# Reordering the first tiles of a layer-norm stage: one maximum earlier, one later, one product-weight step on GpSimd

## Chip, cores and metric

One core of a Trainium2 chip runs the whole program. The metric is the device time of one execution in microseconds. The median of three runs of the kernel before is 331.34 us (331.23 to 331.82).

## What is computed

The reference has three stages; only the last one is touched. x (3072 x 512) is what the two stages ahead (chunked attention, then a soft mixture of experts) give.

```python
h = x @ w_in                                   # 3072 x 1024
e = np.exp(h - h.max(-1, keepdims=True))
sm = e / (e.sum(-1, keepdims=True) + 1e-09)
solu = h * sm
mu = solu.mean(-1, keepdims=True)
var = ((solu - mu) ** 2).mean(-1, keepdims=True)
ln = (solu - mu) / np.sqrt(var + 1e-06) * g_ln
return ln @ w_out                              # 3072 x 512
```

## The kernel before

The last stage works on 24 tiles of 128 tokens, numbered from 0. For every tile the steps are these; the names in italics are used from here on, and a number behind them in brackets is the tile.

- *h*: two products of 512 columns on TensorE (L659), into one of two PSUM pairs h0 and h1, by turns. A pair is free again when *u* of the tile two before has read it.
- *max* on VectorE (L665), *e* (the exponential, with its sum) on ScalarE (L668), *u* (h times e, with its sum) on VectorE (L674).
- *y*, the affine step that takes the mean off: on VectorE for tiles 1 and 2 (L688), halves on VectorE and ScalarE for tile 0 (L688, L692), on GpSimd for tile 3 (L690), on ScalarE from tile 4 on (L694).
- *sq* on ScalarE (L697), then *var* and *rstd* on GpSimd (L701 to L713, eleven small instructions), for the scale of the output row.
- y has to be transposed. For tiles 0 to 3 TensorE does it (L716, eight products into the PSUM tile t). From tile 4 on y goes through DRAM: a *store* of 512 KB (L722), four *fetch* transfers of 128 KB (L727), both issued on SP, and a *turning* on VectorE (L730).
- The transposed y is split into a high part, *hi* on ScalarE (L737), and a low part, *lo* on VectorE (L741), for accuracy.
- The *products* (L747): 24 of 128 x 512 per tile into one PSUM bank, eight of them yh by w_out's high part (whi), eight yh by its low part (wlo), eight yl by whi. The first ten of a tile are five pairs (whi, wlo); the eleventh is the first that needs lo.
- *out* on ScalarE (L765) and a write of 256 KB on SP (L766).

w_out comes in eight blocks. Each is unpacked by seven steps, of which the last two are the high part on ScalarE (L636) and the low part on VectorE (L640); the eighth block's steps are the entries `l` of the hand-written list `TAIL`, which orders the work up to tile 0's low parts. Behind it the function `final` orders everything: each step gets a time (`FRONT[n]` plus an offset of `OFF` for the steps up to y and the statistics, `HS[n]` for h, `begin[n]`, from which the products of a tile start, for the rest), and the steps are issued in the order of these times. The times are only sort keys; an engine takes its own instructions in that order, and waits for others by semaphores. An instruction that waits holds up all that stand behind it on its engine, on SP as well. Tiles beyond the tables get `front` from `begin` less `LEAD`.

Lines that matter: L52 and L53 (the tables), L57 (the list), L629 to L643 (the steps of w_out), L775 to L820 (`final`).

Of the kernel before, what the change touches and what calls it, by code (L numbers as in the profile page):

```python
# [7 lines left out]
FP32 = mybir.dt.float32  # L8
# [5 lines left out]
ALU = mybir.AluOpType  # L14
# [19 lines left out]
FC = FF // P  # L34
# [14 lines left out]
NCONST = 425  # L49
NPE, NZ = 4, 4  # L50
T0, TPE, TDM, TF, LEAD, TT, TO, TH = 6.2, 6.85, 5.51, 3.0, 16.3, 3.8, 6.3, 2.2
FRONT = (0.0, 5.5, 8.1, 15.5, 15.1)  # L52
HS = (0.0, 1.2999999999999998, 4.8, 10.3, 12.9)  # L53
YON = 'daddp'
OFF = {'max': 0.25, 'e': 1.7, 'u': 3.3, 'y': 3.6, 'sq': 5.25, 'var': 5.75, 'rstd': 10.0, 'yt': -2.6, 'hi': -2.1, 'lo': -0.1, 'st': 3.65, 'fe': 7.75, 'tr': 0.0, 'hi2': 0.45, 'lo2': 3.95, 'mh': 0.68, 'ml0': 3.4, 'ml': 0.21, 'l0': 0.7, 'l1': 7.25}

TAIL = (  # L57
    "so open l l l min l l e12 ha hb max s0 s1 t0 e keep w0 u t1 y0 y1 l w1 yt0 hi0 yt1 hi1 lo0 l lo1 e3"
).split()

SPR = ("pp", "ap")
# [17 lines left out]
def tile_kernel(ctx: ExitStack, tc: tile.TileContext, kr, vr, w1, w2, w_in, w_out, cst, out):  # L79
    nc = tc.nc  # L80
    pe, dve, act, pool, sp = nc.tensor, nc.vector, nc.scalar, nc.gpsimd, nc.sync
# [60 lines left out]
    g_sb = at("cst", C_G, FC)  # L142
# [22 lines left out]
    whi, wlo = {}, {}  # L165
# [336 lines left out]
    def c4t(i):  # L502
        return at(f"c4t{i // 12}", i % 12 * P, P, FP32R)
# [125 lines left out]
    def wout_ops(j, t):  # L629

        w = wo[t % len(wo)]

        def hi():
            area(f"w{j}", [(f"wh{j}", DM), (f"wl{j}", DM)])
            whi[j], wlo[j] = at(f"wh{j}", 0, DM, FP32R), at(f"wl{j}", 0, DM, FP32R)
            act.activation(out=whi[j], in_=w, func=ACTF.Copy, scale=g_sb[:, j:j + 1])  # L636

        return cast_ops(slot_of["wout", j], at("tmp", 512 * (t % 2), 512), w, dve) + [
            hi,
            lambda: dve.scalar_tensor_tensor(  # L640
                out=wlo[j], in0=w, scalar=g_sb[:, j:j + 1], in1=whi[j].bitcast(FP32), op0=ALU.mult, op1=ALU.subtract
            ),
        ]  # L643
# [7 lines left out]
    def sc(name, i):  # L651
        k = ("nm", "s", "nu", "vs", "x", "t", "r").index(name)
        o = 64 + 16 * (i % 8) + k
        return small[:, o:o + 1]

    def emit_h(i, halves=(0, 1)):
        for half in halves:
            sl = slice(512 * half, 512 * half + 512)
            pe.matmul(  # L659
                out=fin["h"][i % 2][:, sl], lhsT=c4t(i) if i else at("c0", 0, P), rhs=m4[:, sl] if i else mps[:, sl],  # L660
                start=True, stop=True,
            )
# [112 lines left out]
    def final():  # L775

        steps = []

        def put(t, f, *args):
            steps.append((t, len(steps), f, args))  # L780

        begin = [T0]
        for n in range(NTILE):
            begin.append(begin[-1] + (TPE if n + 1 < NPE else TDM))
        front = list(FRONT)
        for n in range(len(front), NTILE):
            front.append(max(front[-1] + TF, begin[n] - LEAD))
        for n in range(NTILE):
            a, b = front[n], begin[n]
            w = OFF  # L790
            if n >= 1:
                put(HS[n] if n < len(HS) else a - TH, emit_h, n)
                put(a + w["max"], emit_max, n)
                put(a + w["e"], emit_e, n)
                put(a + w["u"], emit_u, n)
                put(a + w["y"], emit_y, n)
            put(a + w["sq"], emit_sq, n)
            put(a + w["var"], emit_var, n)
            put(a + w["rstd"], emit_rstd, n)
            if 1 <= n < NPE:  # L800
                for f in range(FC):
                    put(b + w["yt"], emit_yt, n, f)
                put(b + w["hi"], emit_hi, n)
                put(b + w["lo"], emit_lo, n)
            if n >= NPE:
                put(a + w["st"], emit_store, n)
                put(a + w["fe"], emit_fetch, n)
                put(b - TT + w["tr"], emit_turned, n)
                put(b - TT + w["hi2"], emit_hi, n)
                put(b - TT + w["lo2"], emit_lo, n)  # L810
            if n == NTILE - 1:
                put(b + w["l0"], emit_last, n, 0)
                put(b + w["l1"], emit_last, n, 1)
                continue
            for f in range(FC):
                put(b + w["mh"] * f, main_hi, n, f)
                put(b + w["ml0"] + w["ml"] * f, main_lo, n, f)
            put(b + TO, emit_out, n)
        for t, _, f, args in sorted(steps, key=lambda x: x[:2]):
            f(*args)  # L820

    with tc.manual_schedule():
# [34 lines left out]
        for j in range(NEARLY):  # L857
# [4 lines left out]
            out=sel, in_=ident.rearrange("p (t s) -> p t s", t=4)[:, 0:GT, :], axis=AX.X, op=ALU.add  # L862
# [125 lines left out]
        def e3():  # L988
# [3 lines left out]

        bufs = {}
        last = wout_ops(FC - 1, 1)
        calls = dict(
            so=m_so, open=open_final, min=m_in, l=lambda: last.pop(0)(),
        )
        first = TAIL.index("e12")
        for x in TAIL[:first]:
# [3 lines left out]
        ob = [at("ob", 512 * i, 512) for i in range(3)]  # L1003
        sq = at("sq", 0, 1024)
        calls.update(
            h0=lambda: emit_h(0), ha=lambda: emit_h(0, (0,)), hb=lambda: emit_h(0, (1,)), max=lambda: emit_max(0), s0=lambda: m_sum(0), s1=lambda: m_sum(1),
            keep=lambda: keep_clock(fin["o"][1], KEEP[3]), t0=lambda: m_top(0), t1=lambda: m_top(1),
            w0=lambda: m_low(0), w1=lambda: m_low(1), e=lambda: emit_e(0), u=lambda: emit_u(0),
            y0=lambda: emit_y(0, 0), y1=lambda: emit_y(0, 1),
            yt0=lambda: [emit_yt(0, f) for f in range(4)], yt1=lambda: [emit_yt(0, f) for f in range(4, 8)],  # L1010
            hi0=lambda: emit_hi(0, 0), hi1=lambda: emit_hi(0, 1), lo0=lambda: emit_lo(0, 0), lo1=lambda: emit_lo(0, 1),
            e3=e3,
# [71 lines left out]
```

## Time and profile before

| what | value |
|---|---|
| median of three runs | 331.34 us |
| the profiled execution | 331.76 us |
| its span, first to last instruction | 330.0 us |
| TensorE busy | 298.8 us (91%) |
| VectorE busy | 236.9 us (72%) |
| ScalarE busy | 222.5 us (67%) |
| GpSimd busy | 169.1 us (51%) |
| granted TensorE clock | 1.00 |
| products L747 | 552, 129.8 us, mean 390 ns |

The last stage fills the time from about 174 us to the end. A product's 390 ns is its latency; products follow each other faster than that. Idle time of an engine only costs something where TensorE has to wait for it.

### The profile page before, as it was taken

The numbers are of one execution on the slowest core, as the hardware profiler recorded it, in microseconds if no ns is written. First come the engines' busy times: TensorE is split into PE (matmuls) and PEld (weight loads), VectorE is DVE, ScalarE is ACT, GpSimd is POOL, SyncE is SP. The second block draws the span as 40 slices with busy tenths as digits, with TensorE's granted clock in tenths as the row PEclk, the third lists the DMA queues.
The fourth block names the chain that finished last, engine by engine and source line by source line (L and its number), as shares of the span: only waits on it lengthen the run. The fifth ranks groups of instructions, "written<-read, shape, count | busy, mean of one in ns | idle before, by whom it ended". The sixth has DMA issues, their size and how long they took to land.

```text
span 330.0 us, 8289 instructions
## 1 busy us (share of the span) xinstructions
PE 298.8 (91%) x3069; PEld 217.0 (66%) x3069; DVE 236.9 (72%) x431; ACT 222.5 (67%) x441; POOL 169.1 (51%) x395
## 2 busy tenths in 40 slices
PE   2787989898898799879899899999999999999996
PEld 2576767677676433333335688888888888888885
DVE  6675888886877339998027986888878788787540
ACT  3566756865775446785326789998888888888721
POOL 5255577666675022233100457777767676666600
PEclk9999999999999999999999999999999999999999
DMA  7999999999999999999930005675656756576521
GB/s 291 422 368 411 412 415 420 413 420 414 416 403 412 392 422 428 422 423 423 422 148 0 1 34 195 240 264 199 234 218 219 251 203 219 219 237 238 194 95 65
DMA packets 32696, 95.85 MB, mean 290 GB/s; under 512 B 3856, under 2 KB 14480, under 8 KB 28944
## 3 DMA queue, kind: packets, MB, share of 16 engines
q1 hardware_dynamic: 32512, 95.11, 74.0%
q8 instruction: 24, 0.39, 0.5%
q10 hardware_dynamic: 144, 0.22, 0.2%
q14 instruction: 16, 0.13, 0.1%
HBM read 78.53 MB, written 16.78 MB: 289 GB/s over the span
## 4 chain that ended last, share of the span: by engine, by line
PE 61%; DMA 18%; DVE 9%; POOL 3%; issue 3%; ACT 2%; SPq 1%; POOLq 0%; ACTq 0%; DVEq 0%
PE bank L747 37%; DMA kq_area<-in_kr_dram 9%; DMA ex_area<-in_w_dram 5%; PE bank L281 5%; PE bank L337 4%; DMA e_area<-in_w_dram 4%; PE h L659 4%; POOL kq_area L330 3%; PE bank L319 2%; SPq L201 1%; PE bank L348 1%; PE bank L360 1%; PE bank L407 1%; PE bank L524 1%; PE bank L757 1%
## 5 line engine op out<-in xcount | busy, mean ns | idle before, releaser
L747 PE MATMUL bank<-wh_area,yh_area 128*128 128x512 f32 x552 | 129.8, 390 | 0.0
L747 PEld LDWEIGHTS bank<-wh_area,yh_area 128*128 128x128 f32 x552 | 103.4, 188 | 21.7
L330 POOL TENSOR_SCALAR kq_area<-kq_area 64x416 f32<-64x416 f32 x88 | 38.3, 440 | 36.2 <-DMA kq_area<-in_kr_dram 21.1
L281 PE MATMUL bank<-kq_area 128*32 128x128 f32 x768 | 29.4, 288 | 14.3 <-POOL kq_area L330 7.3
L322 ACT COPY s_area<-bank 128x384 f32<-128x384 f32 x32 | 15.3, 477 | 32.7 <-PE bank L319 31.4
L730 DVE STREAM_TRANSPOSE yq_area<-yq_area 128x1024 f32<-128x1024 f32 x20 | 24.9, 1245 | 17.2 <-DMA yq_area<-z 17.2
L674 DVE SCALAR_TENSOR_TENSOR eb_area<-h,eb_area 128x1024 f32<-128x1024 f32 x24 | 29.1, 1217 | 9.5 <-ACT eb_area L668 9.2
L281 PEld LDWEIGHTS bank<-kq_area 128*32 128x32 f32 x768 | 20.6, 114 | 20.6 <-POOL kq_area L330 10.7
L299 DVE TENSOR_REDUCE cst_area<-bank 128x6 f32<-128x384 f32 x32 | 17.8, 555 | 19.5 <-PE bank L281 19.0
L337 PE MATMUL bank<-vz_area,s_area 128*32 128x130 f32 x768 | 28.7, 274 | 3.3 <-issue 1.2
L712 POOL TENSOR_SCALAR cst_area<-cst_area 128x1 f32<-128x1 f32 x72 | 26.6, 370 | 7.6
L665 DVE TENSOR_REDUCE cst_area<-h 128x1 f32<-128x1024 f32 x24 | 29.0, 1217 | 0.9 <-PE h L659 0.9
L701 POOL TENSOR_SCALAR cst_area<-cst_area 128x1 f32<-128x1 f32 x24 | 16.9, 705 | 22.4 <-ACT eb_area L668 20.5
L668 ACT ACTIVATE eb_area<-h,cst_area 128x1024 f32<-128x1024 f32 x24 | 26.7, 1112 | 1.9 <-DVE cst_area L665 1.9
L697 ACT ACTIVATE eb_area<-eb_area,cst_area 128x1024 f32<-128x1024 f32 x24 | 27.3, 1139 | 0.1
L694 ACT ACTIVATE eb_area<-eb_area,cst_area 128x1024 f32<-128x1024 f32 x20 | 23.1, 1154 | 4.8 <-DVE eb_area L674 4.3
L741 DVE TENSOR_TENSOR yh_area<-yq_area,yh_area 128x1024 fp32r<-128x1024 f32 x20 | 24.5, 1226 | 2.3 <-ACT yh_area L737 2.3
L337 PEld LDWEIGHTS bank<-vz_area,s_area 128*32 128x32 f32 x768 | 21.6, 108 | 5.8 <-issue 2.2
L737 ACT CAST yh_area<-yq_area 128x1024 fp32r<-128x1024 f32 x20 | 21.0, 1049 | 5.4 <-DVE yq_area L730 5.3
L713 POOL TENSOR_SCALAR cst_area<-cst_area 128x1 f32<-128x1 f32 x72 | 19.9, 276 | 7.1
L765 ACT ACTIVATE eb_area<-bank,cst_area 128x512 f32<-128x512 f32 x23 | 15.8, 687 | 9.7 <-POOL cst_area L703 7.0
L314 ACT ACTIVATE s_area<-s_area 128x384 f32<-128x384 f32 x32 | 16.9, 530 | 2.4 <-DVE s_area L305 2.3
(153 smaller groups left out, 526.9 us busy)
## 6 DMA issues: line engine op xcount, KB each, us to landing
e_area<-in_w_dram SPq DMA_DIRECT2D x15, 1024.0 KB, 10.4
kq_area<-in_kr_dram SPq DMA_DIRECT2D x32, 400.0 KB, 7.3
vz_area<-in_vr_dram SPq DMA_DIRECT2D x32, 390.0 KB, 6.6
ex_area<-in_w_dram SPq DMA_DIRECT2D x10, 1024.0 KB, 14.8
z<-eb_area SPq DMA_DIRECT2D x20, 512.0 KB, 2.8
yq_area<-z SPq DMA_DIRECT2D x80, 128.0 KB, 2.9
out_dram<-eb_area SPq DMA_DIRECT2D x23, 256.0 KB, 2.0
e_area<-in_w_in_dram SPq DMA_DIRECT2D x4, 1024.0 KB, 9.0
```

The costliest lines, as they stand in the source:

```text
L281: pe.matmul(out=bk[32 * j:32 * j + 32, t * 128:(t + 1) * 128], lhsT=kq[i][:, KT + c * CH:KT + (c + 1) * CH], rhs=kwin(g % 2, c), start=Tru ...
L330: pool.tensor_scalar(out=o, in0=i, scalar1=1.0, scalar2=0.0, op0=ALU.mult, op1=ALU.add)
L337: pe.matmul(out=bk[32 * j:32 * j + 32, t * 2 * VW:(t + 1) * 2 * VW], lhsT=atb[g % 2][:, c * CH:(c + 1) * CH], rhs=vz[g // 2 % 2][:, :, g % ...
L665: dve.tensor_reduce(out=sc("nm", i), in_=fin["h"][i % 2], axis=AX.X, op=ALU.max, negate=True)
L668: act.activation(out=eb[i % FIN], in_=fin["h"][i % 2], func=ACTF.Exp, bias=sc("nm", i), accum_out=sc("s", i))
L674: dve.scalar_tensor_tensor(out=ub[i % FIN], in0=fin["h"][i % 2], scalar=-1.0 / FF, in1=eb[i % FIN], op0=ALU.mult, op1=ALU.mult, accum_out= ...
L694: act.activation(out=yb[i % FIN], in_=ub[i % FIN], func=ACTF.Identity, scale=-float(FF), bias=sc("nu", i))
L697: act.activation(out=sq, in_=ub[i % FIN], func=ACTF.Square, scale=-float(FF), bias=sc("nu", i), accum_out=sc("vs", i))
L712: pool.tensor_scalar(out=t, in0=r, scalar1=r, scalar2=xx, op0=ALU.mult, op1=ALU.mult)
L730: dve.transpose(out=yv[i % FIN].rearrange("p (f a t) -> p a f t", f=FC, a=4), in_=yq[i % FIN].rearrange("p (a f t) -> p a f t", f=FC, a=4),)
L741: dve.tensor_tensor(out=yl[i % FIN][:, sl], in0=tps(i, sl) if i < NPE else yv[i % FIN], in1=yh[i % FIN][:, sl].bitcast(FP32), op=ALU.subtract,
L747: pe.matmul(out=fin["o"][i % 2], lhsT=a[i % FIN][:, f * 128:(f + 1) * 128], rhs=w[f], start=start, stop=stop)
```

## The change

It changes the two tables and the list, and adds one function.

- `max` of tile 1 leaves `final` and stands in the list (`h1 x1`) ahead of tile 0's two low parts.
- The last two steps of w_out's eighth block (`l l`) move up behind `e12`, and the low part of that block is done on GpSimd, by a multiplication and a subtraction (`low`), where VectorE did it in one instruction.
- `FRONT` moves tile 2 from 8.1 to 9.7, tile 3 from 15.5 to 16.6 and tile 4 from 15.1 to 16.0, and gives tile 5, which had 21.47 by the rule, 23.0.
- `HS` moves the products h of tile 4 from 12.9 to 16.1 and those of tile 5 from 19.27 to 23.1.

```diff
-FRONT = (0.0, 5.5, 8.1, 15.5, 15.1)
-HS = (0.0, 1.2999999999999998, 4.8, 10.3, 12.9)
+FRONT = (0.0, 5.5, 9.7, 16.6, 16.0, 23.0)
+HS = (0.0, 0.0, 4.8, 10.3, 16.1, 23.1)
 TAIL = (
-    "so open l l l min l l e12 ha hb max s0 s1 t0 e keep w0 u t1 y0 y1 l w1 yt0 hi0 yt1 hi1 lo0 l lo1 e3"
+    "so open l l l min l l e12 l l ha hb max s0 s1 t0 e keep w0 u t1 y0 y1 w1 yt0 hi0 yt1 hi1 h1 x1 lo0 lo1 e3"
 ).split()
...
-            lambda: dve.scalar_tensor_tensor(
+            lambda: low(w, j) if j == FC - 1 else dve.scalar_tensor_tensor(
                 out=wlo[j], in0=w, scalar=g_sb[:, j:j + 1], in1=whi[j].bitcast(FP32), op0=ALU.mult, op1=ALU.subtract
             ),
         ]
+
+    def low(w, j):
+        pool.tensor_scalar(out=w, in0=w, scalar1=g_sb[:, j:j + 1], scalar2=0.0, op0=ALU.mult, op1=ALU.add)
+        pool.tensor_tensor(out=wlo[j], in0=w, in1=whi[j].bitcast(FP32), op=ALU.subtract)
...
-            if n >= 1:
+            if n >= 2:
                 put(HS[n] if n < len(HS) else a - TH, emit_h, n)
                 put(a + w["max"], emit_max, n)
+            if n >= 1:
                 put(a + w["e"], emit_e, n)
...
-max=lambda: emit_max(0), s0=
+max=lambda: emit_max(0), h1=lambda: emit_h(1), x1=lambda: emit_max(1), s0=
```

Since the times are sort keys, other steps change places too. The line numbers of the changed kernel are four higher in these functions.

On VectorE, from the start of tile 1 on, before (L665 max, L741 lo, L640 the low part of w_out, L674 u, L688 y; h1 is tile 1 and then tile 3, h0 is tile 2 and then tile 4):

```order
L741 TENSOR_TENSOR yh_area_2268<-bank1_85,yh_area_2268 128x512
L640 SCALAR_TENSOR_TENSOR wh7_area_2292<-wo2_area_1823,cst_area_66,wh7_area_2292 128x512
L741 TENSOR_TENSOR yh_area_2268<-t_2248,yh_area_2268 128x512
L665 TENSOR_REDUCE cst_area_66<-h1_2250 128x1
L665 TENSOR_REDUCE cst_area_66<-h0_2249 128x1
L674 SCALAR_TENSOR_TENSOR eb_area_2269,cst_area_66<-h1_2250,eb_area_2269 128x1024
L688 TENSOR_SCALAR eb_area_2269<-eb_area_2269,cst_area_66 128x4x8x32
L674 SCALAR_TENSOR_TENSOR eb_area_2269,cst_area_66<-h0_2249,eb_area_2269 128x1024
L688 TENSOR_SCALAR eb_area_2269<-eb_area_2269,cst_area_66 128x4x8x32
L741 TENSOR_TENSOR yh_area_2268<-t_2248,yh_area_2268 128x1024
```

and now, on VectorE from tile 1's maximum to the low part of tile 3 (the last row; L669 max, L678 u, L692 y, L745 lo):

```order
L669 TENSOR_REDUCE cst_area_66<-h1_2250 128x1
L745 TENSOR_TENSOR yh_area_2268<-bank1_85,yh_area_2268 128x512
L745 TENSOR_TENSOR yh_area_2268<-t_2248,yh_area_2268 128x512
L678 SCALAR_TENSOR_TENSOR eb_area_2269,cst_area_66<-h1_2250,eb_area_2269 128x1024
L692 TENSOR_SCALAR eb_area_2269<-eb_area_2269,cst_area_66 128x4x8x32
L669 TENSOR_REDUCE cst_area_66<-h0_2249 128x1
L745 TENSOR_TENSOR yh_area_2268<-t_2248,yh_area_2268 128x1024
L678 SCALAR_TENSOR_TENSOR eb_area_2269,cst_area_66<-h0_2249,eb_area_2269 128x1024
```

Tile 1's maximum moved ahead of the two half-width low parts, tile 2's maximum behind tile 1's y, and tile 2's u behind tile 1's low part. Further down on VectorE u of tile 5 still stands ahead of lo of tile 3.

On ScalarE, around the high part of tile 3 (L737), before (L668 e of tile 5, L694 y, L765 out, L697 sq):

```order
L697 ACTIVATE eb_area_2269,cst_area_66<-eb_area_2269,cst_area_66 128x1024 x2
L668 ACTIVATE eb_area_2269,cst_area_66<-h1_2250,cst_area_66 128x1024
L737 CAST yh_area_2268<-t_2248 128x1024
L694 ACTIVATE eb_area_2269<-eb_area_2269,cst_area_66 128x1024
L765 ACTIVATE eb_area_2269<-bank0_84,cst_area_66 128x512
```

and now on ScalarE (L741 the high part, L672 e, L769 out, L698 y, L701 sq):

```order
L701 ACTIVATE eb_area_2269,cst_area_66<-eb_area_2269,cst_area_66 128x1024 x2
L741 CAST yh_area_2268<-t_2248 128x1024
L672 ACTIVATE eb_area_2269,cst_area_66<-h1_2250,cst_area_66 128x1024
L769 ACTIVATE eb_area_2269<-bank0_84,cst_area_66 128x512
L698 ACTIVATE eb_area_2269<-eb_area_2269,cst_area_66 128x1024
```

The exponential of tile 5 moved behind the high part of tile 3, and its y behind out of tile 2.

On SP, at tiles 5 and 6 before (z1 is tile 5's copy in DRAM, z2 tile 6's, z3 tile 7's; L722 store, L727 fetch, L766 the write of an output tile):

```order
L722 DMA z1_2232<-eb_area_2269 128x1024
L766 DMA out_0_dram<-eb_area_2269 128x512
L727 DMA yq_area_2308<-z1_2232 32x4x256 x4
L722 DMA z2_2233<-eb_area_2269 128x1024
L766 DMA out_0_dram<-eb_area_2269 128x512
L727 DMA yq_area_2308<-z2_2233 32x4x256 x4
```

and now on SP (L726 store, L731 fetch, L770 output):

```order
L770 DMA out_0_dram<-eb_area_2269 128x512
L726 DMA z1_2232<-eb_area_2269 128x1024
L726 DMA z2_2233<-eb_area_2269 128x1024
L731 DMA yq_area_2312<-z1_2232 32x4x256 x4
L770 DMA out_0_dram<-eb_area_2269 128x512
L731 DMA yq_area_2312<-z2_2233 32x4x256 x4
```

The store of tile 6 moved ahead of the fetch of tile 5. On TensorE h of tile 4 moved from between the last product of tile 0 and the first of tile 1 to behind ten products of tile 1, and h of tile 5 in the same way from ahead of tile 2's products to behind ten of them; h of tile 3 keeps its place behind 18 products of tile 0.

## Rows read from the trace of the kernel before

**Rows 1.** Windows: length, busy us (PE, PEld, DVE, ACT, POOL), clock, DMA share, GB/s

```profile
185.00:190.00 5.00, 4.15 (x23) 3.11 (x22) 4.56 (x7) 4.19 (x7) 2.91 (x9) 1.00 0.00 0
280.00:300.00 20.00, 20.00 (x89) 16.52 (x88) 15.82 (x17) 16.85 (x25) 12.92 (x38) 1.00 0.63 224
```

**Rows 2.** Timeline of TensorE, tiles 0 and 1: start, us, what, [idle before it]

```profile
181.00 1.17 PE L659 MATMUL h<-m_area,c4t_area 128*128 128x512 f32 x4
182.00 4.26 PE L747 MATMUL bank<-wh_area,yh_area 128*128 128x512 f32 x18
...
187.10 0.73 PE L659 MATMUL h<-m_area,c4t_area 128*128 128x512 f32 x2 [0.85 <-DVE eb_area L674]
...
187.67 0.39 PE L747 MATMUL bank<-wh_area,yh_area 128*128 128x512 f32 x1
...
187.90 1.09 PE L716 MATMUL t<-cst_area,eb_area 128*128 128x128 f32 x8
...
190.43 4.49 PE L747 MATMUL bank<-wh_area,yh_area 128*128 128x512 f32 x19
```

**Rows 3.** Timeline of VectorE and ScalarE, the same stretch

```profile
183.33 2.35 DVE L665 TENSOR_REDUCE cst_area<-h 128x1 f32<-128x1024 f32 x2
...
184.58 1.12 ACT L668 ACTIVATE eb_area<-h,cst_area 128x1024 f32<-128x1024 f32 x1 [1.52 <-DVE cst_area L665]
...
185.82 1.23 DVE L674 SCALAR_TENSOR_TENSOR eb_area<-h,eb_area 128x1024 f32<-128x1024 f32 x1
...
187.09 0.75 DVE L688 TENSOR_SCALAR eb_area<-eb_area,cst_area 128x1024 f32<-128x1024 f32 x1
...
189.03 1.02 ACT L737 CAST yh_area<-t 128x1024 fp32r<-128x1024 f32 x1 [0.70 <-PE t L716]
...
190.08 1.23 DVE L741 TENSOR_TENSOR yh_area<-t,yh_area 128x1024 fp32r<-128x1024 f32 x1 [0.31 <-ACT yh_area L737]
...
191.22 2.35 DVE L665 TENSOR_REDUCE cst_area<-h 128x1 f32<-128x1024 f32 x2
```

**Rows 4.** Groups of GpSimd by form: count, busy us, mean ns, idle before

```profile
L619 POOL TENSOR_TENSOR cst_area<-cst_area 128x512 f32<-128x512 f32 x8 | 10.4, 1297 | 0.7
...
L690 POOL TENSOR_SCALAR eb_area<-eb_area,cst_area 128x1024 f32<-128x1024 f32 x1 | 1.1, 1118 | 0.1
```

**Rows 5.** Timeline, tile 3's high and low part, products of tiles 3, 4, 5

```profile
202.64 1.02 ACT L737 CAST yh_area<-t 128x1024 fp32r<-128x1024 f32 x1 [0.67 <-PE t L716]
...
203.69 1.23 DVE L741 TENSOR_TENSOR yh_area<-t,yh_area 128x1024 fp32r<-128x1024 f32 x1 [0.39 <-ACT yh_area L737]
...
204.05 3.12 PE L747 MATMUL bank<-wh_area,yh_area 128*128 128x512 f32 x13
...
213.38 5.62 PE L747 MATMUL bank<-wh_area,yh_area 128*128 128x512 f32 x24
```

**Rows 6.** Timeline: fetch of tile 5, y and store of tile 6, turning of tile 5

```profile
207.41 1.74 SPq L727 DMA_DIRECT2D yq_area<-z  x4
...
208.80 1.15 ACT L694 ACTIVATE eb_area<-eb_area,cst_area 128x1024 f32<-128x1024 f32 x1 [0.36 <-DVE eb_area L674]
...
209.98 0.34 SPq L722 DMA_DIRECT2D z<-eb_area  x1
...
211.63 1.25 DVE L730 STREAM_TRANSPOSE yq_area<-yq_area 128x1024 f32<-128x1024 f32 x1 [0.59 <-DMA yq_area<-z]
```

**Rows 7.** Timelines of SP and VectorE: a fetch behind an output write, its turning

```profile
246.42 0.36 SPq L766 DMA_DIRECT2D out_dram<-eb_area  x1
246.87 1.83 SPq L727 DMA_DIRECT2D yq_area<-z  x4
...
252.35 1.25 DVE L730 STREAM_TRANSPOSE yq_area<-yq_area 128x1024 f32<-128x1024 f32 x1 [1.32 <-DMA yq_area<-z]
```

**Rows 8.** Waits of SP, 180 to 330 us: total us, times, longest

```profile
SPq L722 <- ACT eb_area L694: 25.2, 20, 6.6
```

**Rows 9.** Window near the program's start, columns as in Rows 1

```profile
14.00:16.00 2.00, 0.40 (x7) 0.17 (x9) 1.07 (x3) 1.15 (x4) 0.81 (x2) 1.00 1.04 408
```

More of the change, by code (lines that the diff above doesn't have):

```diff
@@ L1005, in tile_kernel @@
         calls.update(
-            h0=lambda: emit_h(0), ha=lambda: emit_h(0, (0,)), hb=lambda: emit_h(0, (1,)), max=lambda: emit_max(0), s0=lambda: m_sum(0), s1=lambda: m_sum(1),
+            h0=lambda: emit_h(0), ha=lambda: emit_h(0, (0,)), hb=lambda: emit_h(0, (1,)), max=lambda: emit_max(0), h1=lambda: emit_h(1), x1=lambda: emit_max(1), s0=lambda: m_sum(0), s1=lambda: m_sum(1),
             keep=lambda: keep_clock(fin["o"][1], KEEP[3]), t0=lambda: m_top(0), t1=lambda: m_top(1),
```

## The prediction

> **What bounds the kernel now.** I read the windows first. TensorE is busy for 20.00 of 20 us late in the program and for only 4.15 of 5 us between 185 and 190 [rows 1]. So from about 190 us on the products on TensorE are the bound, and only a hole in TensorE's row of work can be won there or lost there. The timeline of TensorE shows the one hole of that stretch: the pair of products for the maximum of tile 3, h(3), stands behind 18 products of tile 0 and waits 0.85 us for VectorE [rows 2]. One product costs (4.26 - 0.39) / 17 = 0.228 us when they follow each other [rows 2]. The 18 leave the array free at 182.00 + 18 x 0.228 = 186.10; the waiting pair starts at 187.10 and the next product follows after 0.57 instead of 2 x 0.228 = 0.46 [rows 2]. The hole is therefore 1.00 + 0.11 = 1.11 us, and I charge every later wait in the same way: moment of release plus 0.11.
>
> The timeline of VectorE and ScalarE shows what h(3) waits for: its PSUM pair is held until u(1) (L674, tile 1) has read it. u(1) starts at 185.82, 1.24 behind e(1), which is 1.25 behind max(1) at 183.33 [rows 3]. Three operations stand in front of max(1): the two low halves of tile 0 and the low part of the last w_out block. The same rows give the pitch of a full queue: lo(1) at 190.08 lasts 1.23 and the next starts 1.14 later, 0.09 before its end [rows 3]; I take 1.14 for a queued operation of VectorE and 1.02 - 0.1 = 0.9 for a high part on ScalarE.
>
> **Part 1, tile 1's maximum ahead of the low parts; w_out's low part to GpSimd.** The products for h(1) and h(2) start at 181.00 and last 1.17 [rows 2], so h(1), the first pair, ends at about 182.17 - 0.46 = 181.7. max(1) can start there, 1.63 earlier than 183.33. Then u(1) starts at 185.82 - 1.63 = 184.2 and h(3) is free 1.28 later (187.10 less 185.82) [rows 2, 3] at 185.5, before TensorE asks at 186.10. Even a square of tile 0 that holds e(1) up by 0.5 would be hidden. Gain: 1.11 us. The two low halves of tile 0 move behind max(1), to 182.9; the first, of half lo(1)'s length, is over by 183.6, and the eleventh product of tile 0 needs it at 182.00 + 10 x 0.228 = 184.3, so they stay hidden. On GpSimd the low part is two instructions: a tensor_scalar over 512 columns, at most the 1.12 us that one over 1024 takes, and a tensor_tensor of 512 at 1.30 [rows 4]. At most 2.4 us, from about 176 on; hi7, the first product that reads the result, comes after 186. Cost nothing, and still nothing at three times the price. The high part that moves ahead on ScalarE lies in its wait for the products of the summed w_in rows.
>
> **Part 2, tile 2's maximum behind tile 1's affine step, products of tiles 4 and 5 later.** h(4) now follows ten products of tile 1, and h(5) ten of tile 2. In before h(4) lay between the last product of tile 0 and the first of tile 1, and hid tile 1's high part (L737). From the first transpose of tile 1 to the first product of tile 1 is 190.43 - 187.90 = 2.53 us [rows 2], 2.07 without h(4). The high part starts 1.13 behind the transposes, lasts 1.02 [rows 2, 3], and is released with some 0.05: 2.20 + 0.11 = 2.31. Stall: 0.24 us, and the same again at tile 2. I take 0.24 each; ends 0 (the weight load slips in as it does now) and 0.35. In times: hi(1) at 189.03 - 1.11 = 187.92, first product of tile 1 at 189.10. e(2) now stands behind hi(1) on ScalarE and u(2) behind lo(1) on VectorE: u(2) at 187.92 + 1.05 + 1.14 = 190.11, free for h(4) at 191.39; TensorE asks at 189.10 + 2.28 = 191.38. Stall about 0.1, and again 0.1 at h(5) behind u(3). What is left of the gain by the transposes of tile 3 is 1.11 - 0.48 - 0.20 = **0.43 us**.
>
> **Part 3, what the later plan does to tile 3 and tile 5.** ScalarE now has hi(3) ahead of e(5), and on VectorE u(5) stands, as before, ahead of lo(3). hi(3) starts at 202.64 - 0.43 = 202.21 [rows 5]. e(5) follows 0.9 later at 203.11, u(5) 1.24 later at 204.35, lo(3) 1.15 later at 205.50 (queued), and it ends 1.23 later at 206.73. In before lo(3) started at 203.69 [rows 5]. TensorE's first product that needs it is the eleventh of tile 3: 204.05 - 0.43 + 2.28 = 205.90. Release 206.73 + 0.05 + 0.11 = 206.89: a stall of **0.99 us**. TensorE is then 0.56 us later than before.
>
> **Part 4, the queue of SP.** Now store(6) is issued ahead of fetch(5), both on SP. SP is a program that waits: it spent 25.2 us waiting for the affine step before its stores [rows 8]. So fetch(5) now waits for y(6). The chain: lo(3) 205.50, max(6) 206.64 (+1.14), e(6) 207.89 (+1.25), u(6) 209.13 (+1.24), y(6) 210.40 (+1.27, as u(1) to y(1) in rows 3), store(6) 211.58 (+1.18, 208.80 to 209.98 in rows 6), fetch(5) 211.94 (+0.36). In before fetch(5) went at 207.41 [rows 6]. From fetch to the turning of the tile on VectorE (L730): 4.22 us here [rows 6]; 5.48 where a 256 KB write was issued 0.45 ahead [rows 7]. Now a 512 KB store is issued 0.36 ahead. I take 5.0, between the two and nearer to the second, whose queue looks most like it. Then: turning 216.94, hi(5) 1.28 later at 218.22, its end and release 219.29, first product 219.40. TensorE is ready for tile 5 at 213.38 + 11 x 0.228 = 215.89 in before (the first 11 of the 24 are tile 4's) [rows 5], 216.45 now. Stall **2.95 us** (2.17 with 4.22, 3.43 with 5.48).
>
> The Trainium skill (DMA: Bandwidth & Descriptors, Queues, rings and completion order) says that each DMA engine takes the descriptors of one ring in order. By it the fetch's data stand behind the store's 512 KB; at the 224 GB/s that the windows show on average that would be up to 2.3 us, an estimate, and the sum would be near 336.4. The trace has no fetch right behind a store, so it neither bears this out nor excludes it.
>
> **Sum.** -1.11 + 0.48 + 0.20 + 0.99 + 2.95 = +3.51 us. From there on nothing gives it back: TensorE is full late in the program [rows 1]. For tile 6 I reckon no further wait, since its turning becomes late by about as much as its products do; this is the least certain step. The profiled execution took 331.76 with a span of 330.0; it would take 335.27. The median is 0.42 below that execution: **334.9 us**. With 4.22 for the fetch 334.1, with 5.48 335.3; and as 5.48 - 4.22 = 1.26 stood behind a 256 KB write, a store twice as large may cost 2.52: 336.6.
>
> **Rivals.** (a) *The fetch is not held* (on the other side). Decided at the turning of tile 5: if it starts by about 213.9, hi(5) is there when TensorE's weight load asks, and part 4 costs nothing. For it: store(5) itself goes early, at 204.35 + 1.27 + 1.18 = 206.8. Against it: the order on SP, and its waits in rows 8. Then -1.11 + 0.68 + 0.99 = +0.56: 331.9, no change. (b) *Neither lo(3) nor the fetch binds*, since ScalarE and VectorE run further ahead than I reckon; it needs lo(3) 1.0 us earlier. Then -0.43: 330.9, no change; without the stalls of 0.24 and 0.1 as well, -1.11: 330.2, faster. (c) *The clock falls* in the hole of 3 us before tile 5. TensorE had 0.40 us of work in the two microseconds from 14 to 16 and the granted clock stayed 1.00, the 2.4 GHz level [rows 9]; no row shows the lower level. At 1.2 GHz the 24 products of one tile (5.46) would take 5.5 us more: near 340. The Trainium skill (TensorE: Matmul & The Clock Gate, Part 1) has idleness lower the clock; this trace, with its short holes, shows no such fall.
>
> **Chances.** Forecast 0.80 (334.1 to 336.6); (a) 0.08; (b) 0.08, of it 0.03 faster; (c) 0.04. A measurement of this kernel tells some 0.2%, 0.66 us, from no change. Slower 0.84, same 0.13, faster 0.03. The range reaches a little beyond the forecast's own to both sides for stalls at tiles 3 and 5 that are shorter than reckoned or go on to tile 6: 333.0 to 336.8.
>
> **What would show it.** Right: h(3) without a wait near 186.1; short waits before the first products of tiles 1 and 2 for the high part; a wait of about 1 us at the eleventh product of tile 3 for lo(3); a wait of 2 to 3.5 us before tile 5's first product, with fetch(5) issued right behind store(6) near 212; then TensorE full to the end. Wrong: a fetch(5) near 208, u(5) long before hi(3)'s end, or a clock under 1.00 behind 216 us.

## The result and the profile after

The changed kernel took 335.43 us in the median of six runs (334.26 to 337.33), the kernel before 331.28 (330.94 to 331.82) beside it: a ratio of 1.0113 with a 95% interval of 1.0077 to 1.015. It is slower by 4.2 us, where 334.9 with a range of 333.0 to 336.8 was forecast. The profiled execution took 335.31 us with a span of 333.5. Lines of the code after the new helper stand four lower than before: h is L663, the maximum L669, e L672, u L678, the products L751, the store L726, the fetch L731, the turning L734, high parts L741, low parts L745, the transposes on TensorE L720.

The windows come first, columns as in [rows 1]. Between 185 and 190 us TensorE is now full, where 4.15 of 5 us stood before. Two new holes stand later, and late in the program it is full as before:

```profile
185.00:190.00 5.00, 5.00 (x27) 3.94 (x26) 3.48 (x4) 3.89 (x6) 2.22 (x8) 1.00 0.00 0
205.00:210.00 5.00, 4.22 (x19) 3.13 (x18) 4.88 (x8) 4.50 (x7) 3.27 (x12) 1.00 0.39 157
215.00:220.00 5.00, 1.94 (x9) 1.31 (x8) 3.07 (x4) 1.71 (x2) 3.30 (x12) 1.00 0.68 190
219.00:221.00 2.00, 1.70 (x7) 1.42 (x8) 2.00 (x4) 1.92 (x3) 0.26 (x1) 1.00 0.00 0
225.00:300.00 75.00, 75.00 (x332) 61.88 (x331) 61.57 (x66) 65.24 (x92) 49.98 (x146) 1.00 0.65 229
```

The timeline of TensorE (start, duration, line, count, idle before and its releaser) answers [rows 2, 5]. The holes are those of two tiles:

```profile
181.49 4.26 PE L751 MATMUL bank<-wh_area,yh_area 128*128 128x512 f32 x18
185.58 0.62 PE L663 MATMUL h<-m_area,c4t_area 128*128 128x512 f32 x2
...
186.27 1.04 PE L720 MATMUL t<-cst_area,eb_area 128*128 128x128 f32 x8
187.06 3.91 PE L751 MATMUL bank<-wh_area,yh_area 128*128 128x512 f32 x15
190.81 0.73 PE L663 MATMUL h<-m_area,c4t_area 128*128 128x512 f32 x2
...
193.44 1.03 PE L720 MATMUL t<-cst_area,eb_area 128*128 128x128 f32 x8
...
200.64 1.03 PE L720 MATMUL t<-cst_area,eb_area 128*128 128x128 f32 x8
...
203.12 2.45 PE L751 MATMUL bank<-wh_area,yh_area 128*128 128x512 f32 x10
206.36 0.97 PE L751 MATMUL bank<-wh_area,yh_area 128*128 128x512 f32 x3 [0.78 <-DVE yh_area L745]
...
207.62 5.65 PE L751 MATMUL bank<-wh_area,yh_area 128*128 128x512 f32 x24
...
213.57 2.67 PE L751 MATMUL bank<-wh_area,yh_area 128*128 128x512 f32 x11
219.30 3.24 PE L751 MATMUL bank<-wh_area,yh_area 128*128 128x512 f32 x13 [3.06 <-ACT yh_area L741]
```

h(3) runs behind its 18 products without a wait. Tile 3's products stop before the eleventh, for the low part; tile 5's stop before the first, for its high part. What tile 5 waits for is read in the timelines of SP, VectorE and ScalarE, which answer [rows 6]:

```profile
206.37 5.10 SPq L726 DMA_DIRECT2D z<-eb_area  x2
211.52 2.19 SPq L731 DMA_DIRECT2D yq_area<-z  x4
...
216.93 1.25 DVE L734 STREAM_TRANSPOSE yq_area<-yq_area 128x1024 f32<-128x1024 f32 x1 [4.72 <-DMA yq_area<-z]
...
218.21 1.04 ACT L741 CAST yh_area<-yq_area 128x1024 fp32r<-128x1024 f32 x1 [4.29 <-DVE yq_area L734]
```

The two stores of the first line are those of tiles 5 and 6; the second is issued at about 211.1 (206.37 + 5.10 is its end) and the fetch right behind it. Before, the fetch went at 207.41, ahead of the store [rows 6]. What tile 3 waits for is read on VectorE, u(5) and behind it lo(3):

```profile
203.93 1.22 DVE L678 SCALAR_TENSOR_TENSOR eb_area<-h,eb_area 128x1024 f32<-128x1024 f32 x1 [3.95 <-POOL cst_area L717]
...
205.08 1.22 DVE L745 TENSOR_TENSOR yh_area<-t,yh_area 128x1024 fp32r<-128x1024 f32 x1
```

The size of every experiment below is taken from the last stage alone: from the first product of tile 0 to the last output step on ScalarE. That leaves out the stages ahead of it, which no edit touches save by the early steps of w_out (see the last experiment) and whose length moves the start by some microseconds from one execution to the next: from 180.90 to 185.53 us in the profiles here. Each kernel has one profile unless more are named. A median below comes with its ratio to the kernel before as it ran beside it, whose median was then 331.32 to 332.25 us, and with the ratio's 95% interval in brackets; the ratio is the recorded one and not quite the quotient of the two medians. Those last steps are, of the kernel after and then of the kernel before:

```profile
330.41 0.47 ACT L765 ACTIVATE eb_area<-bank,cst_area 128x256 f32<-128x256 f32 x1 [1.69 <-PE bank L761]
```

```profile
326.86 0.47 ACT L761 ACTIVATE eb_area<-bank,cst_area 128x256 f32<-128x256 f32 x1 [1.69 <-PE bank L757]
```

After: 330.41 - 181.49 = 148.92. Before: 326.86 - 182.00 [rows 2] = 144.86. The stage grew by **4.06 us**; the span by 3.5, since the stage happened to start 0.51 earlier in this execution.

### The profile page after: what moved, and what is told of

It reads as the page before. It is cut to its first block, busy times and chain, and to the rows that moved or that the text cites. A ratio compares the mean times of both kernels' runs of the same rounds, so it can differ in the third digit from the quotient of the medians.

```text
span 333.5 us, 8291 instructions
## 1 busy us (share of the span) xinstructions
PE 300.5 (90%) x3069; PEld 217.4 (65%) x3069; DVE 238.3 (71%) x430; ACT 222.3 (67%) x441; POOL 167.8 (50%) x397
## 4 chain that ended last, share of the span: by engine, by line
PE 55%; DMA 17%; DVE 13%; ACT 5%; POOL 4%; issue 3%; SPq 1%; POOLq 0%; ACTq 0%; DVEq 0%
PE bank L751 31%; DMA kq_area<-in_kr_dram 5%; DMA ex_area<-in_w_dram 5%; PE bank L281 4%; PE bank L337 4%; DMA e_area<-in_w_dram 4%; PE h L663 3%; DMA w_area<-in_w_out_dram 2%; PE bank L319 2%; POOL kq_area L330 2%; DVE eb_area L678 1%; PE bank L360 1%; PE bank L407 1%; PE bank L348 1%; DMA yq_area<-z 1%
## 5 line engine op out<-in xcount | busy, mean ns | idle before, releaser
L751 PE MATMUL bank<-wh_area,yh_area 128*128 128x512 f32 x552 | 131.0, 391 | 3.8 <-ACT yh_area L741 3.1
L751 PEld LDWEIGHTS bank<-wh_area,yh_area 128*128 128x128 f32 x552 | 103.1, 188 | 27.1 <-ACT yh_area L741 4.2
L734 DVE STREAM_TRANSPOSE yq_area<-yq_area 128x1024 f32<-128x1024 f32 x20 | 24.9, 1244 | 21.9 <-DMA yq_area<-z 21.9
L678 DVE SCALAR_TENSOR_TENSOR eb_area<-h,eb_area 128x1024 f32<-128x1024 f32 x24 | 29.0, 1209 | 8.4 <-ACT eb_area L672 4.2
L669 DVE TENSOR_REDUCE cst_area<-h 128x1 f32<-128x1024 f32 x24 | 29.1, 1217 | 2.7 <-PE h L663 2.7
L716 POOL TENSOR_SCALAR cst_area<-cst_area 128x1 f32<-128x1 f32 x72 | 26.1, 363 | 7.6
L741 ACT CAST yh_area<-yq_area 128x1024 fp32r<-128x1024 f32 x20 | 21.0, 1051 | 13.3 <-DVE yq_area L734 13.3
L701 ACT ACTIVATE eb_area<-eb_area,cst_area 128x1024 f32<-128x1024 f32 x24 | 27.4, 1140 | 2.1 <-DVE eb_area L678 2.0
L717 POOL TENSOR_SCALAR cst_area<-cst_area 128x1 f32<-128x1 f32 x72 | 24.1, 334 | 7.1
L672 ACT ACTIVATE eb_area<-h,cst_area 128x1024 f32<-128x1024 f32 x24 | 26.6, 1110 | 0.9 <-DVE cst_area L669 0.9
L745 DVE TENSOR_TENSOR yh_area<-yq_area,yh_area 128x1024 fp32r<-128x1024 f32 x20 | 24.5, 1227 | 2.3 <-ACT yh_area L741 2.3
L698 ACT ACTIVATE eb_area<-eb_area,cst_area 128x1024 f32<-128x1024 f32 x20 | 23.1, 1154 | 4.5 <-DVE eb_area L678 3.8
L707 POOL TENSOR_SCALAR cst_area<-cst_area 128x1 f32<-128x1 f32 x24 | 6.4, 268 | 27.3 <-ACT eb_area L701 26.9
L769 ACT ACTIVATE eb_area<-bank,cst_area 128x512 f32<-128x512 f32 x23 | 15.7, 681 | 5.5 <-POOL cst_area L707 3.3
```

Of the source, the lines that this page charges most:

```text
L672: act.activation(out=eb[i % FIN], in_=fin["h"][i % 2], func=ACTF.Exp, bias=sc("nm", i), accum_out=sc("s", i))
L678: dve.scalar_tensor_tensor(out=ub[i % FIN], in0=fin["h"][i % 2], scalar=-1.0 / FF, in1=eb[i % FIN], op0=ALU.mult, op1=ALU.mult, accum_out= ...
L701: act.activation(out=sq, in_=ub[i % FIN], func=ACTF.Square, scale=-float(FF), bias=sc("nu", i), accum_out=sc("vs", i))
L716: pool.tensor_scalar(out=t, in0=r, scalar1=r, scalar2=xx, op0=ALU.mult, op1=ALU.mult)
L717: pool.tensor_scalar(out=r, in0=t, scalar1=1.5, scalar2=r, op0=ALU.add, op1=ALU.mult)
L734: dve.transpose(out=yv[i % FIN].rearrange("p (f a t) -> p a f t", f=FC, a=4), in_=yq[i % FIN].rearrange("p (a f t) -> p a f t", f=FC, a=4),)
```

## The experiments

The theory is the sum of the prediction, with its sizes as now read, each between the same two steps of both kernels. Of the kernel before this takes three rows of TensorE more:

```profile
194.76 1.04 PE L716 MATMUL t<-cst_area,eb_area 128*128 128x128 f32 x8
...
201.57 1.03 PE L716 MATMUL t<-cst_area,eb_area 128*128 128x128 f32 x8
...
207.47 5.62 PE L747 MATMUL bank<-wh_area,yh_area 128*128 128x512 f32 x24
```

- From the first product to tile 1's transposes: 4.78 us (186.27 - 181.49) where it was 5.90, so **-1.12** for h(3).
- From tile 1's transposes to tile 2's 7.17 where it was 6.86, and on to tile 3's 7.20 where it was 6.81: **+0.31** and **+0.39** for the uncovered high parts and the waits for u. In the 15 products at 187.06, 3.91 us long, 0.33 is wait (14 x 0.228 + 0.39 = 3.58 without one); the kernel before lost 0.14 there too (2.53 less 0.46 for h(4) is 2.07 us, for what takes 0.79 + 5 x 0.228 = 1.93), so the cost against it is less.
- From tile 3's first product to tile 4's: 4.50 (207.62 - 203.12) where it was 3.42, so **+1.08** for lo(3). Of this 0.96 is the wait itself (206.36 less 203.12 + 2.28).
- Over tile 4 **+0.04**, and **+3.22** before tile 5 (219.30 less 213.57 + 2.51). The 13 products behind that hole take 3.24 where they took 3.11 (5.62 - 2.51): **+0.13**.

Together that is +4.05 of the 4.06. The rivals were that the wait for GpSimd that the trace names before u(5) holds lo(3), not e(5) behind hi(3); that the moved list part gains nothing by itself; and that the low part on GpSimd delays VectorE beside it.

**Tile 5's fetch ahead of tile 6's store again**, in the changed kernel:

```diff
-                put(a + w["fe"], emit_fetch, n)
+                put(a + w["fe"] - (0.2 if n == 5 else 0), emit_fetch, n)
```

> The changed kernel with one thing put back: on SP the fetch of tile 5 goes ahead of the store of tile 6. Theory (the order on SP makes the 3.2 us hole before tile 5's products): fetch(5) near 209, the hole falls to 0.3 us or less, the wait of 1 us for lo(3) stays, time about 332.1, 0.8 over the kernel before. Rival (tile 5 is late in any case, since its own e, u and y are late): the hole stays at 2 us or more and the time at 334 or more.

The stage is 145.60, +0.74 against before; the terms without tile 5's give -0.42 + 1.08 + 0.04 = +0.70. The median is 332.39, a ratio of 1.001 (0.9979 to 1.0041). The profiled execution was the slowest of the ten, 336.04, since its stage started only at 185.53. TensorE runs tile 5's 24 products in one piece; tile 3's wait stays:

```profile
210.39 0.96 PE L751 MATMUL bank<-wh_area,yh_area 128*128 128x512 f32 x3 [0.79 <-DVE yh_area L745]
...
217.56 5.62 PE L751 MATMUL bank<-wh_area,yh_area 128*128 128x512 f32 x24
```

```profile
213.03 1.74 SPq L731 DMA_DIRECT2D yq_area<-z  x4
215.18 0.34 SPq L726 DMA_DIRECT2D z<-eb_area  x1
```

From fetch to turning (217.30) it takes 4.27 us here and 216.93 - 211.52 = 5.41 behind the store, and the four fetches take 1.74 to issue instead of 2.19. Two issues on SP in the other order are 148.92 - 145.60 = 3.32 of the 4.06 us.

**e(5) ahead of hi(3) again**, in the changed kernel:

```diff
-                put(a + w["e"], emit_e, n)
+                put(a + w["e"] - (0.2 if n == 5 else 0), emit_e, n)
```

> The changed kernel with e(5) ahead of hi(3) on ScalarE, and nothing else; the fetch of tile 5 stays behind the store of tile 6. Theory (u(5) waits for an e(5) that stands behind hi(3), and lo(3) waits behind u(5)): the wait of about 1 us at tile 3's eleventh product goes, the store of tile 6 goes some 2 us earlier, the hole before tile 5 shrinks to about 2 us, time about 333.3. Rival (u(5) is held by GpSimd's small instructions, to which the trace puts down its wait of 3.95 us): u(5) stays near 203.9, the wait of 1 us stays, time within 0.4 of the changed kernel's 335.4.

The stage is 146.93, +2.07, where the terms give -0.42 + 2.37 + 0.13 = +2.08. The wait for the low part is gone, and the hole before tile 5 shrinks to 218.35 - (213.47 + 2.51) = 2.37, since the whole chain to store(6) moved up with u(5):

```profile
204.14 3.12 PE L751 MATMUL bank<-wh_area,yh_area 128*128 128x512 f32 x13
...
213.47 2.67 PE L751 MATMUL bank<-wh_area,yh_area 128*128 128x512 f32 x11
218.35 3.24 PE L751 MATMUL bank<-wh_area,yh_area 128*128 128x512 f32 x13 [2.21 <-ACT yh_area L741]
```

On VectorE, u(5) now waits for e(5) and not for GpSimd, and starts 1.24 us ahead of tile 3's first product, where it was 0.81 behind it. So it was ScalarE's order that held it, though the trace of the changed kernel named GpSimd:

```profile
202.90 1.23 DVE L678 SCALAR_TENSOR_TENSOR eb_area<-h,eb_area 128x1024 f32<-128x1024 f32 x1 [1.88 <-ACT eb_area L672]
```

The median of four runs, 336.02 (1.0114; 1.0073 to 1.0154), is higher than this profiled execution (334.36) and missed the expectation. The other three had a lower mean clock, 0.99 against 0.995, but no trace that would show where it fell. What a fall costs, the next kernel shows.

**The other way round: the kernel before with that one fetch late.**

```diff
-                put(a + w["fe"], emit_fetch, n)
+                put(a + w["fe"] + (1.5 if n == 5 else 0), emit_fetch, n)
```

> The kernel before with one thing of the change: on SP the fetch of tile 5 goes behind the store of tile 6. Theory: fetch(5) near 210.4 in place of 207.4; if the store's data stand in front of it, turning 5.4 later and a hole of 2.3 us, time 333.6; if they don't, turning 4.2 later and a hole of 1.2, time 332.5. Rival (the order on SP alone costs nothing, because tile 5 has cover): 331.3.

334.71 us, 1.0095 (1.0061 to 1.013): the order of one fetch and one store makes the kernel before nearly as slow as the changed one. But the stage grew by 3.97 (148.83), more than the hole of 217.36 - (212.60 + 2.51) = 2.25. The 13 products behind it take 4.82 us instead of the 3.24 of the changed kernel. TensorE's row and the windows (the column before the last two is the granted clock) say why:

```profile
212.60 2.67 PE L747 MATMUL bank<-wh_area,yh_area 128*128 128x512 f32 x11
217.36 4.82 PE L747 MATMUL bank<-wh_area,yh_area 128*128 128x512 f32 x13 [2.09 <-ACT yh_area L737]
```

```profile
218.00:219.00 1.00, 1.00 (x4) 0.81 (x3) 1.00 (x2) 1.00 (x2) 0.00 (x0) 0.50 0.00 0
221.00:222.00 1.00, 1.00 (x6) 0.82 (x5) 0.62 (x1) 1.00 (x3) 0.73 (x3) 1.00 0.68 262
```

Behind the hole the granted clock was 0.50, the 1.2 GHz level, and 1.00 again from 221 on: 1.58 us on top of the hole. The Trainium skill (TensorE: Matmul & The Clock Gate, Part 1) has idleness of TensorE lower its clock; this row agrees. In the profile of the changed kernel the clock was 1.00 behind a longer hole (the windows at the head). It did fall elsewhere in that execution, near the program's start, behind two microseconds with 0.16 us of work:

```profile
14.00:16.00 2.00, 0.16 (x8) 0.16 (x12) 0.76 (x3) 1.20 (x4) 0.81 (x2) 1.00 1.05 415
18.00:20.00 2.00, 2.00 (x22) 1.62 (x25) 0.62 (x2) 1.27 (x4) 1.68 (x5) 0.50 1.02 412
```

Eight of the thirteen profiles show a fall there, between 15 and 23 us, and one more shows one near 122; the kernel before shows none, so [rows 9] told only what that one execution did. The last stage does not start later for it: at 180.90 to 182.52 us in seven of the eight and at 185.53 in one, against 181.89 to 182.75 in the other five. Three more runs followed.

**The changed kernel twice more, and the late fetch in the kernel before once more**, with no other edit:

> The changed kernel, unaltered, beside the kernel before on this chip, for the spread of its time. Theory (after the hole before tile 5 the clock is sometimes halved for a while, as in the profile of the kernel before with the late fetch, where it cost 1.6 us): profiles of the changed kernel show either 148.9 us from the first product of tile 0 to the last output at a full clock, or about 150.5 with a granted clock of 0.5 behind the hole; time 334.3 to 337. Rival (the spread has nothing to do with the hole): every profile shows a full clock behind the hole and 148.9.

> The same kernel once more, for a third profile: 148.9 us from the first product of tile 0 to the last output with a full clock behind the hole before tile 5, about 150.5 with a halved one.

> The kernel before with the fetch of tile 5 behind the store of tile 6 once more. Theory: the hole before tile 5's products is 2.3 us again; the clock behind it is halved as in the first profile or it is not, and then the stretch from the first product to the last output is 147.2 us in place of 148.8. Rival (the halved clock belongs to this kernel): 148.8 again.

The first gave 337.53 (four runs; 1.017, 1.0112 to 1.0229) and a stage of 151.86, +7.00 and more than the 150.5 expected. The hole is 218.96 - (212.96 + 2.51) = 3.49, and the 13 products behind it take 5.92. The clock was down before they began, and longer than in the kernel above. TensorE's row, then the windows:

```profile
212.96 2.67 PE L751 MATMUL bank<-wh_area,yh_area 128*128 128x512 f32 x11
218.96 5.92 PE L751 MATMUL bank<-wh_area,yh_area 128*128 128x512 f32 x13 [3.33 <-ACT yh_area L741]
```

```profile
218.00:219.00 1.00, 0.04 (x1) 0.04 (x1) 1.00 (x3) 0.92 (x2) 0.55 (x3) 0.50 0.10 23
219.00:221.00 2.00, 2.00 (x5) 1.63 (x6) 2.00 (x2) 2.00 (x2) 0.00 (x0) 0.50 0.00 0
223.00:225.00 2.00, 2.00 (x7) 1.59 (x6) 2.00 (x3) 1.64 (x2) 1.69 (x4) 0.56 0.67 188
225.00:227.00 2.00, 2.00 (x10) 1.64 (x9) 1.57 (x2) 1.52 (x3) 1.41 (x5) 1.00 0.89 302
```

The second had its hole (2.99 us of wait) and no fall of the clock: 334.9 us, stage +4.01. In the kernel before with the late fetch the clock fell again (335.84 us, stage +3.83):

```profile
213.63 2.67 PE L747 MATMUL bank<-wh_area,yh_area 128*128 128x512 f32 x11
218.22 4.84 PE L747 MATMUL bank<-wh_area,yh_area 128*128 128x512 f32 x13 [1.92 <-ACT yh_area L737]
```

```profile
220.00:222.00 2.00, 2.00 (x6) 1.52 (x6) 1.71 (x2) 2.00 (x4) 1.01 (x4) 0.50 0.65 265
```

The sums, each against the stage's growth. The first column is how much later than before the last 11 products of tile 4 start, counted from the first product of tile 0 (31.38 us in before, 213.38 - 182.00); the third is what the 13 products behind the hole take beyond 3.11, with the clock's share of it (what they take beyond 3.24) in brackets:

| kernel | ahead of the hole | hole before tile 5 | products behind it | sum | stage grew by |
|---|---|---|---|---|---|
| after, first profile | +0.70 | 3.22 | 0.13 | 4.05 | 4.06 |
| after, second | +0.68 | 3.49 | 2.81 (2.68) | 6.98 | 7.00 |
| after, third | +0.68 | 3.15 | 0.17 | 4.00 | 4.01 |
| after, fetch(5) first | +0.65 | 0 | 0 | 0.65 | 0.74 |
| after, e(5) first | -0.43 | 2.37 | 0.13 | 2.07 | 2.07 |
| before, fetch(5) late | +0.01 | 2.25 | 1.71 (1.58) | 3.97 | 3.97 |
| before, fetch(5) late, again | +0.01 | 2.08 | 1.73 (1.60) | 3.82 | 3.83 |

The hole's length alone does not decide whether the clock falls: it did behind 2.08, 2.25 and 3.49, and not behind 2.37, 3.15 and 3.22. What does is left open.

**Both tables without their new last entries**, to undo the orders of tiles 3 and 5 while keeping the rest:

```diff
-FRONT = (0.0, 5.5, 9.7, 16.6, 16.0, 23.0)
-HS = (0.0, 0.0, 4.8, 10.3, 16.1, 23.1)
+FRONT = (0.0, 5.5, 9.7, 16.6, 16.0)
+HS = (0.0, 0.0, 4.8, 10.3, 12.9)
```

> The changed kernel with the entries of tiles 4 and 5 as they were: no sixth entry of the first table, h of tile 4 at 12.9 and of tile 5 by the rule. Tile 1's maximum, w_out's low part on GpSimd, tile 2's later maximum and tiles 3 and 4 at 16.6 and 16.0 stay. Theory (the gain of 1.1 is real and all the loss comes from the moves of h(4), h(5) and tile 5): h(3) without a wait, at most one short wait of 0.25 at tile 3's first product, time 330.2 to 330.5. Rival (the early maximum or GpSimd's part costs elsewhere what it gains): 331.3 or more.

333.71 (1.0061; 1.0031 to 1.009), stage +1.52: a miss. The edit changes the computation. The keys order the data too: h(4) at 12.9 is now issued ahead of u(2) at 9.7 + 3.3, in the PSUM pair that u(2) still has to read, and h(5) ahead of u(3), so that u(2) and u(3) read the products of tiles 4 and 5. TensorE waits 1.06 us for e at both places. What it shows is only why the change had to move h(4) and h(5) once tiles 2 and 3 had moved.

**Tile 5's front 0.13 earlier**, which puts both orders back and keeps the two h where the change has them:

```diff
-FRONT = (0.0, 5.5, 9.7, 16.6, 16.0, 23.0)
+FRONT = (0.0, 5.5, 9.7, 16.6, 16.0, 22.87)
```

> The changed kernel with one number: the sixth entry of the first table 22.87 in place of 23.0, which puts both e(5) ahead of hi(3) on ScalarE and the fetch of tile 5 ahead of the store of tile 6 on SP. Measured from the first product of tile 0 to the last output step, which was 144.86 us in the kernel before and 148.92 in the changed one. Theory (the two orders are all of the loss beyond the uncovered high parts): no wait at tile 3's eleventh product, none over 0.3 us before tile 5; what stays is the 1.11 us gained at h(3) less 0.9 for two high parts and two waits for u: 144.6, the time within 0.4 us of the kernel before. Rival (moving tile 5 by 1.5 us costs in itself): 145.5 or more.

331.26 (0.9992; 0.9963 to 1.0022), stage 144.50: -0.36, against -0.42 by the terms that stay (-1.12 + 0.31 + 0.39). Tiles 3 and 5 run without a wait, and the fetch at 208.16 is followed by its turning at 212.62, 4.46 later. One number in the table, 23.0 for 22.87, is what makes the changed kernel slow.

**The same, with h(3) behind tile 1's transposes**, so that it covers tile 1's high part:

```diff
-FRONT = (0.0, 5.5, 9.7, 16.6, 16.0, 23.0)
-HS = (0.0, 0.0, 4.8, 10.3, 16.1, 23.1)
+FRONT = (0.0, 5.5, 9.7, 16.6, 16.0, 22.87)
+HS = (0.0, 0.0, 4.8, 10.5, 16.1, 23.1)
```

> The same number 22.87, and the products h(3) at 10.5 in place of 10.3, which puts them behind the transposes of tile 1, so that they hide its high part. Theory (the wait of 0.33 before tile 1's first product is the high part without cover): that wait is gone, first product of tile 0 to last output 144.3 us, 0.6 under the kernel before. Rival (that wait has another cause, such as the transposes themselves or tile 1's y): it stays or moves in front of the transposes, 144.6 or more.

Stage 144.14, -0.72; median 331.66 (0.9972; 0.9943 to 1.0001). The 15 products now take 3.58, so the 0.33 of the uncovered high part is gone:

```profile
188.46 3.58 PE L751 MATMUL bank<-wh_area,yh_area 128*128 128x512 f32 x15
```

**The list part alone, and the low part on GpSimd alone**, in the kernel before with its old tables. The first has max(1) early, the last two steps of w_out's eighth block moved up, and its low part on GpSimd. The second leaves max(1) where it was and has only this:

```diff
-    "so open l l l min l l e12 ha hb max s0 s1 t0 e keep w0 u t1 y0 y1 l w1 yt0 hi0 yt1 hi1 lo0 l lo1 e3"
+    "so open l l l min l l e12 l l ha hb max s0 s1 t0 e keep w0 u t1 y0 y1 w1 yt0 hi0 yt1 hi1 lo0 lo1 e3"
...
-            lambda: dve.scalar_tensor_tensor(
+            lambda: low(w, j) if j == FC - 1 else dve.scalar_tensor_tensor(
...
+    def low(w, j):
+        pool.tensor_scalar(out=w, in0=w, scalar1=g_sb[:, j:j + 1], scalar2=0.0, op0=ALU.mult, op1=ALU.add)
+        pool.tensor_tensor(out=wlo[j], in0=w, in1=whi[j].bitcast(FP32), op=ALU.subtract)
```

> The kernel before with only the list's part of the change: tile 1's maximum ahead of the two low parts, the last low part of w_out on GpSimd; both tables as before, so tile 2's maximum still stands ahead of u(1) on VectorE. Theory (u(1) is what h(3) waits for, and tile 2's maximum ahead of it costs 1.1 us of VectorE's time): the wait of h(3) shrinks from 1.11 to 0.65 us and no other appears: 144.3 us from the first product to the last output, time 0.5 us under the kernel before. Rival (the early maximum alone brings the whole gain, and tile 2's later maximum nothing): 143.8.

> The kernel before with only w_out's last low part on GpSimd; tile 1's maximum stays behind the two low parts. Theory (VectorE's 0.66 us for that step stood in the chain to u(1), and GpSimd's two instructions are hidden): the wait of h(3) shrinks by 0.6 us, the stretch before tile 0's first product is as long as before, 144.2 us from the first product to the last output. Rival (GpSimd's two instructions slow VectorE down at tile 0): the stretch from the first w_in product to tile 0's first product grows beyond its 10.12 us.

Stages 144.27 (-0.59) and 144.21 (-0.65); medians 331.29 (0.9988; 0.9957 to 1.002) and 330.8 (0.9969; 0.9938 to 1.0). The rows of the second, TensorE and then VectorE:

```profile
171.66 1.92 PE L569 MATMUL bank<-cst_area 128*32 128x512 f32 x16 [0.38 <-DVE cst_area L563]
...
181.79 4.29 PE L750 MATMUL bank<-wh_area,yh_area 128*128 128x512 f32 x18
186.22 0.73 PE L662 MATMUL h<-m_area,c4t_area 128*128 128x512 f32 x2
```

```profile
182.45 2.35 DVE L668 TENSOR_REDUCE cst_area<-h 128x1 f32<-128x1024 f32 x2
184.93 1.22 DVE L677 SCALAR_TENSOR_TENSOR eb_area<-h,eb_area 128x1024 f32<-128x1024 f32 x1
```

Those of the first:

```profile
186.38 0.73 PE L662 MATMUL h<-m_area,c4t_area 128*128 128x512 f32 x2 [0.19 <-DVE eb_area L677]
```

```profile
183.97 1.22 DVE L668 TENSOR_REDUCE cst_area<-h 128x1 f32<-128x1024 f32 x1
185.10 1.22 DVE L677 SCALAR_TENSOR_TENSOR eb_area<-h,eb_area 128x1024 f32<-128x1024 f32 x1
```

In the second, h(3) starts 4.43 us behind the first product (186.22 - 181.79), where it was 5.10 and where the 18 products take 4.10. It follows the start of u(1) by 1.29, as it did in the kernel before (1.28): TensorE still waits for u(1), by 0.33 and, with the pair's 0.11, by 0.44 instead of 1.11, though the row prints no idle time. In the first it is no better, 186.38 - 181.89 = 4.49, since max(2), at 183.97, still stands ahead of u(1) at 185.10. So w_out's low part on VectorE was about 0.65 of the 1.11, and the early maximum by itself adds nothing to that. The rest is gained only in the kernels that move max(2) behind y(1) as well, and there h(3) starts 4.09 behind the first product. Nor does GpSimd's work cost the stage ahead: from L569 to the first product of tile 0 it takes 10.13 us here, and 10.12 both in before and in the changed kernel. These two and the one with h(3) later have the shortest stages seen; each interval reaches 1, so by the medians none is shown to beat the kernel before, though each stage is 0.6 to 0.7 shorter in its profile.

## Why the prediction was right

**Part 1** held in its size: 1.11 was reckoned and 1.12 came, and h(3) follows its 18 products at 181.49 + 4.09 = 185.58 without a wait. Covered low parts and free GpSimd held too. But Part 1 put the whole gain down to the early maximum and GpSimd's part, and these two alone leave a wait of 0.50 (4.49 - 4.10 and the pair's 0.11). The step that it left out is max(2), which stood between max(1) and u(1) on VectorE; its move was booked in Part 2, as a cost only.

**Part 2** held: 0.34 was reckoned for each of tiles 1 and 2 (0.24 for the uncovered high part, 0.10 for the wait for u), and the two stretches grew by 0.31 and 0.39. The net gain left at tile 3's first product was 0.42 (22.05 - 21.63 us behind the first product), with 0.43 reckoned.

**Part 3** held: 0.99 reckoned, 1.08 measured, and the edit of e(5) alone shows the chain hi(3), e(5), u(5), lo(3).

**Part 4** held in its mechanism: 2.95 was reckoned for tile 5, and 3.22 + 0.13 = 3.35 came in the first profile. The mis-sized step is the fetch behind a store: 5.0 was taken between 4.22 [rows 6] and 5.48 [rows 7]; 5.41 came, near the end measured behind an output write. The further 1.26 for a store of twice the size, which made the upper end 336.6, did not come. The Trainium skill (DMA: Bandwidth & Descriptors, Queues, rings and completion order) says that each DMA engine takes the descriptors of one ring in order; 5.41 behind the store against 4.27 with the fetch ahead of it fits that, but the delay of 1.14 is half of the 2.3 us that was estimated from the store's whole size, and no run tells a wait behind the store's data from a sharing of the engines with them.

**Nothing gives it back**, and no further wait appears at tile 6: the windows behind the hole are full.

**The rivals.** (a), a fetch that is not held, is the kernel with fetch(5) first: 332.39 where 331.9 was given. (b) fell: lo(3) and the fetch both bind. (c) was wrong in its form. It stood as an alternative to the forecast, at 0.04 and 5.5 us, because no row showed the lower clock [rows 9]. It is instead an addition that comes in some executions: in three of the six profiles with such a hole, at 1.6, 1.6 and 2.7 us, since about seven and twelve products ran at half the clock (1.58 / 0.228 and 2.68 / 0.228) and not 24. The spread of the changed kernel's other runs, 334.26 to 337.88, is not shown to come from it, since only the profiled ones have a trace and a run's mean clock does not say where the clock was low: 0.995 stands beside a fall at the program's start alone in the changed kernel's first profile, and beside a fall behind the hole alone in the second of the late fetch. The kernel before spreads too, from 330.20 to 334.38 in 35 runs with mean clocks down to 0.983, and one run of the changed kernel took 336.14 with 1.00. The later median of 337.53 lies above the forecast range; in its profiled execution 2.68 us of the stage's 7.00 are the clock behind the hole.

## What to carry to other kernels

A program that waits in order on a DMA queue makes the place of one line worth microseconds: where keys decide the order, list what each moved key passes on every engine and queue, since 0.13 in one table was worth 4.4 us here (148.92 against 144.50), four times what the edit gained elsewhere. When an operation that an engine waits for is freed, ask what the moved work used to cover (here a high part under h(4)). And a hole in TensorE's row is to be priced with the products behind it, which may run at half the clock for a while.

## What was not expected of the hardware

The clock's fall behind holes of 2 to 3.5 us, in some executions and not in others, with 0.50 granted for some three to seven microseconds; and a like fall near the program's start in eight of thirteen profiles, which cost the last stage nothing that can be seen. And the price of a store just ahead on the same queue: 5.20 to 5.64 us from fetch to turning in six profiles, against 4.22 to 4.46 in seven with the fetch ahead of the store, and 2.15 to 2.20 us instead of 1.74 to issue the four fetches.
